# Three pieces for GpSimd's subtractions, and three later waits, in a fused attention and expert kernel

## The chip, the core and the metric

One Trainium2 chip, of which the program uses one core. The metric is the time of one execution on the device in microseconds (us); three runs of the kernel before are given, and one further execution was taken with the profiler on. The engines are named as in the profile: PE is TensorE (PEld its weight loads), DVE VectorE, ACT ScalarE, POOL GpSimd, and SP SyncE, which issues most transfers.

## The reference

Three layers follow one another, on 4 batches of 576 rows:

```python
# 1: decayed causal attention, 8 heads of 64
scores = scale * q @ k.T + (cum[:, None] - cum[None, :])   # cum: running sum of log f
attn = softmax(where(causal, -1e9, scores))
x = attn @ v                                                # heads side by side: 512 columns
# 2: mixing over rows (rank 32), then a dense layer 512 -> 2048 -> 512
u = x + (x.T @ U @ V).T
y = u + relu(u @ w_ch1) @ w_ch2
# 3: four attention experts of one head each, the best two of four per row
logits = y @ w_gate
out = sum over the chosen e of w[e] * (causal attention of y @ wq[e], y @ wk[e], y @ wv[e]) @ wo[e]
```

## The kernel before

The numbers are kept exact enough by splitting: a float32 operand becomes a high part in a narrower format and a low part that is the rest, and each product is made as high times high, high times low, low times high. So nearly every operand costs a cast on ScalarE (the high part), a subtraction (the low part), and three matmuls.

**First stage, attention (to about 260 us).** 32 heads pass through in slots of 8.4 us, two heads (a pair) per transfer of q and k. The instructions are put in order by a table of times (`put(head, us, what)`), sorted once and written out in that order for all five engines; no engine reorders. Of head h a slot holds: the score products (`sc`, L297) in two halves into the two buffers of the PSUM pool `ps2`; the exponentials (L317, ScalarE, three pieces); the high part `ph` (L322, ScalarE) and the low part (`low_part`, L325, VectorE, both operands in SBUF); the row maxima of the head two slots later (products `ua` L201 and `ub` L219 on TensorE, maxima L206 and L227 on VectorE, their transpose `mt` L233 on TensorE); and the products with the values of the head before (L353 to L357). `ub` uses the PSUM buffer of the second half of the scores, so it needs the last two exponentials done. The groups of the dense stage fill what TensorE has left.

In heads 0 to 9 the causal mask is added by a matmul; from head 10 on (`h >= 2 * NPLAIN`) the exponentials are instead cut off along the diagonal by GpSimd: `affine_select` (L1076), five per head, between the exponential and the cast `ph`. GpSimd has a second task in this stage: `split_low` (L927 to L950). q and k of a head come as float32; ScalarE makes the high parts (L895 to L899), and GpSimd subtracts them, one instruction for q and one for k, each 64 partitions by 576 columns. I call these two a set. A set is put 1.2 us behind its casts, two pairs ahead of its use, and stands in GpSimd's queue in front of the selects of the next head.

**Second stage, dense (to about 550 us).** `ffn_stream` gives groups of twelve matmuls in turn: one of the hidden layer (`hps`, L716), one of the output (`cps`, L732). `hh` (L721, ScalarE) and `hl` (L722, VectorE) make the two parts of a hidden block; `yc` (L738, VectorE) adds an output block to its sum. `hps` and `cps` share three PSUM buffers, taken in turn. Beside this stream runs a list of `jobs`, generators that `dense_one` advances by one `yield` after each group. They read the next quarter of the weights and join its bits (`narrow_quarter`: L461, L462, maximum L528), and find the power of two to scale by (`power`): maximum over columns (L540 for a weight, L592 for u), transpose `amt` on TensorE (L491), three small steps on VectorE on `ar` (L495 to L497), a matmul `rsp` that spreads the number to all partitions (L502), and the factor `es` (L504, L505). Each `yield` between these moves the next step one group later in the order of every engine. `side_factor(q, s, am)` does this for the first (s = 0) and second half of quarter q's weights; it runs for q = 2 and q = 3. `both_sides` then converts the quarter. `prepare_u(b, fy, wait)` issues the loads of batch b's u, waits `wait` groups, takes four maxima (L588), and calls `power`.

**Third stage (to the end).** The four experts; the change touches nothing of it.

Of the kernel before, what the change touches and what calls it, by code (L numbers as in the profile page):

```python
# [15 lines left out]
OP = mybir.AluOpType  # L16
# [3 lines left out]
B, H, S, D = 4, 8, 576, 64  # L20
# [18 lines left out]
UP16 = 4.0  # L39
UPW = 8192.0  # L40
# [38 lines left out]
def f32(ap):  # L79
    return ap.bitcast(F32)  # L80
# [3 lines left out]
def kernel(  # L84
# [13 lines left out]
    nc = tc.nc  # L98
# [4 lines left out]
    def pool(name, bufs=1, side="left", space=None):  # L103
        kw = {} if space is None else {"space": space}
        if space is None:
            kw["side"] = side
            kw["reuse_waits"] = "tile"
        return tc.alloc_tile_pool(name=name, bufs=bufs, **kw)
# [3 lines left out]
    ps2 = pool("ps2", 2, space=PSUM)  # L112
    ps1 = pool("ps1", 1, space=PSUM)
# [68 lines left out]
    cur = {}  # L182
# [5 lines left out]
    def drain(gen):  # L188

        while True:  # L190
            try:
                next(gen)
            except StopIteration as end:
                return end.value
# [15 lines left out]
    where = {3: (0, 0), 0: (0, 448), 2: (1, 0), 1: (1, 320)}  # L210
# [273 lines left out]
        nc.vector.tensor_tensor(back[:], sides[0][:, 0:1], sides[1][:, 0:1], OP.mult)  # L484
        scales[q] = sides, back

    def power(am, up=UP16, where=((ps1, "av"), (ps2, "s2")), pause=None):

        (p0, tag0), (p1, tag1) = where
        at_ = p0.tile([1, P], F32, name="amt", tag=tag0)  # L490
        nc.tensor.transpose(at_[:], am, ident[:])  # L491
        counter[1] += 1
        full = ars[counter[1] % 2]
        ar = full[0:1, :]
        nc.vector.tensor_reduce(ar, at_[:], AX.X, OP.max)  # L495
        nc.vector.tensor_scalar(ar, ar, 1.0e-30, None, OP.max)
        nc.vector.tensor_scalar(ar.bitcast(I32), ar.bitcast(I32), 0x7F800000, None,  # L497
                                OP.bitwise_and)
        yield pause
        yield pause  # L500
        rp = p1.tile([P, 1], F32, name="rsp", tag=tag1)
        nc.tensor.matmul(rp[:], every[:], full[:].bitcast(BF16)[:, 1:2], start=True, stop=True)  # L502
        es = cur["s16"].tile([P, 2], F32, name="es", bufs=16)
        nc.vector.tensor_scalar(es[:, 0:1], rp[:], 1.0 / up, None, OP.mult)  # L504
        nc.vector.reciprocal(es[:, 1:2], es[:, 0:1])  # L505
        return es
# [29 lines left out]
    def side_factor(q, s, am):  # L536

        yield
        a1 = cur["s16"].tile([P, 1], F32, name="wa1", bufs=2)
        nc.vector.tensor_reduce(a1[:], am[:, s, :], AX.X, OP.max)  # L540
        yield
        yield
        sides = scales[q][0]
        sides[s] = yield from power(a1[:], UPW if s else UP16)
        if s:
            back = cur["s16"].tile([P, 1], F32, name="wback", bufs=3)
            nc.vector.tensor_tensor(back[:], sides[0][:, 0:1], sides[1][:, 0:1], OP.mult)
            scales[q][1] = back

    def behind_by_one(pairs):  # L550

        last = None
        for high, low in pairs:
            high()
            if last:
                last()
            last = low
            yield
        last()
        yield  # L560
# [16 lines left out]
    def prepare_u(b, fy, wait=2):  # L577

        us = []
        for c in range(NC):  # L580
            us.append(fy.tile([P, KT, HC], F32, name="ust", tag="yc"))
            nc.sync.dma_start(us[c][:], udram[b, :, :, c * HC:c * HC + HC])
        for _ in range(wait):
            yield
        am = cur["s16"].tile([P, 2 * NC], F32, name="uam", bufs=2)
        for n in range(2 * NC):
            k = 2 * (n % 2)
            nc.vector.tensor_reduce(am[:, n:n + 1], us[n // 2][:, k:k + 2], AX.XY, OP.max,  # L588
                                    apply_absolute_value=True)
            yield  # L590
        a1 = cur["s16"].tile([P, 1], F32, name="ua1", bufs=2)
        nc.vector.tensor_reduce(a1[:], am[:], AX.X, OP.max)  # L592
        yield
        yield
        st_u[b] = us, (yield from power(a1[:]))

    def begin_u(b):

        st_u[b] += tuple(cur["fu"].tile([P, KT, S], F16, name=n + "f", tag=n) for n in ("uh", "ul"))

    def begin_sums(b, ycs):

        us, es, uh, ul = st_u[b]
        for c, yc in enumerate(ycs):
            cs = slice(c * HC, c * HC + HC)
            nc.sync.dma_start(yc[:], ydram[b, :, :, cs])
            for i, step in enumerate(steps):
                if step[:2] == (b, c) and step[2] > 0:
                    loads[i] = uh[:, :, cs], ul[:, :, cs], yc, es
# [10 lines left out]
    def convert_u(b, cs=range(NC)):  # L620
        return [u_parts(b, c, k) for c in cs for k in range(0, KT, 2)]
# [128 lines left out]
    dense, casts, sums, jobs, deferred, late = [], [], {}, [], [], []  # L750

    def ffn_prepare(i):
        if i >= QX1 or i in loads:
            return
        b, c, q, first, head, last = steps[i]
        if not head:
            loads[i] = loads[max(j for j in loads if steps[j][0:2] == (b, c))]
        else:
            loads[i] = ffn_load(b, c, first, cur["fy"])
# [112 lines left out]
    def pair_heads(p):  # L872
        return heads[2 * (p % 2)], heads[2 * (p % 2) + 1]
# [64 lines left out]
    def split_low(p, j, which=(0, 1)):  # L938

        if p >= NPAIR:  # L940
            return
        qa, qb, ka, kb = pair_heads(p)[j]
        tq, tk = places[p % 2][0][:, 0, :], places[p % 2][0][:, 1, :]
        if j == 0:
            todo = ((qb[hi_, :], tq[lo_], qa[lo_, :]), (kb[lo_, :S], tk[lo_], ka[lo_, :S]))
        else:
            todo = ((qb[lo_, :], tq[hi_], qb[hi_, :]), (kb[hi_, :S], tk[hi_], khigh[hi_, :]))
        for n in which:
            dst, src, high = todo[n]
            nc.gpsimd.tensor_tensor(dst, src, f32(high), OP.subtract)  # L950

    def one(gen):

# [489 lines left out]
    def dense_until(i):  # L1443
        while at[0] < i:
            dense_one()

    def dense_to(n):
        while groups[0] < n:
            dense_one()

    del cur["turn"]
    fu, fh, fy = cur["fu"], cur["fh"], cur["fy"]
# [12 lines left out]
    def in_turn(*gens):  # L1465
        for gen in gens:
            yield from gen

    def sums_of(p_, tags):
        return [p_.tile([P, KT, HC], F32, name="yc", tag=n) for n in tags]  # L1470
# [5 lines left out]
    def full_quarter(q, pace):  # L1476

        yield from narrow_quarter(w32[q], q, pace)
        if q == 2:
            both = wy_pool.tile([P, 4, KT, FT * P], F16, name="w16a", tag="a")  # L1480
            W[q] = [both[:, i] for i in range(4)]
        else:
            W[q] = []
            for n in ("w1h", "w1l"):
                one_ = wx_pool.tile([P, 2, KT, FT * P], F16, name=n + "f", tag=n)
                W[q] += [one_[:, i] for i in range(2)]
        jobs.append(both_sides(q))
# [8 lines left out]
    def pauses(n):  # L1496
        for _ in range(n):
            yield

    def first_quarter():  # L1500

        yield from scale_sides(1, largest[1, "sides"])
        yield from convert_weights(1)
# [4 lines left out]
    with tc.manual_schedule(engines=IN_ORDER):  # L1508
        ffn_prepare(NC * (B - 1))
        jobs.append(first_quarter())  # L1510
        jobs.append(prepare_u(0, fy2, 3))
        jobs.append(in_turn(prepare_u(1, fy2, 12)))
        jobs.append(in_turn(pauses(14), full_quarter(2, 2), pauses(8), full_quarter(3, 3)))
        dense_to(8 * (QX1 - 2) + 4)
        begin_u(0)
        begin_sums(0, sums_of(fy2, ("yc", "yc")))
        jobs.append(behind_by_one(convert_u(0)))
        dense_to(8 * (QX1 - 1) + 6)
        begin_u(1)
        jobs.append(behind_by_one(convert_u(1)))  # L1520
        begin_sums(1, sums_of(fy2, ("yc", "yc")))
        dense_until(QX1 + 5)
        jobs.append(prepare_u(2, cur["fy"]))
        dense_until(QX1 + 9)
        begin_u(2)
        begin_sums(2, sums_of(wx_pool, ("w2h", "w2l")))
        jobs.append(in_turn(behind_by_one(convert_u(2)), prepare_u(3, cur["fy"])))
        dense_until(QX1 + 11)
        begin_u(3)
        converts = behind_by_one(convert_u(3))  # L1530
        jobs.append(converts)
        dense_until(QX2)
        drain(converts)
        begin_sums(3, sums_of(cur["fy"], ("yc", "yc")))
        dense_until(QX2 + 3)
        drain(in_turn(*jobs))
        del jobs[:]
# [632 lines left out]
```

## Time and profile before

| | |
|---|---|
| three runs | 784.35, 785.31, 785.93 us (median 785.31) |
| the profiled execution | 784.53 us, of which the span from first to last instruction is 782.8 |
| PE busy | 757.9 us, 97% of the span |
| DVE busy | 601.8 us, 77% |
| ACT busy | 436.4 us, 56% |
| POOL busy | 202.9 us, 26% |
| granted TensorE clock | 0.999 of full speed |

Busy shares are means over the three stages, so they are to be read by stretches. In a timeline a row is: start, duration, engine, line, operation, what is written and read, the shapes, and how many were merged; in brackets how long the engine was idle before and what ended that. Ends of matmuls are modelled, and rows of one engine may overlap by some 0.05 us, since the next instruction starts while the last one drains.

### The profile page before, as it was taken

To read this page: it belongs to the slowest core of one execution; us is meant where nothing else is said; L and a number is where in the kernel's file an instruction comes from. 1 tells how busy PE (TensorE), PEld (TensorE's weight loads), DVE (VectorE), ACT (ScalarE), POOL (GpSimd) and SP (SyncE) were. 2 spreads that over 40 slices of the span, in tenths; PEclk is the share of its full clock that TensorE was granted. 3 is DMA by queue.
4 is the path that set the end of the run, shared out by engine and by line. 5 is a ranking of instruction groups with operands and counts; after the bars stand their busy time and mean duration, and the time that the engine had idled before them with its cause. 6 is when DMAs were issued, how large, how long until landed. Compare 5 with 4: busy or idle time off the path is not lost.

```text
span 782.8 us, 19114 instructions
## 1 busy us (share of the span) xinstructions
PE 757.9 (97%) x7312; PEld 645.3 (82%) x7312; DVE 601.8 (77%) x1662; ACT 436.4 (56%) x892; POOL 202.9 (26%) x357
## 2 busy tenths in 40 slices
PE   8898989999999999999999999999999999999997
PEld 4798989989999999877777777777778888878874
DVE  8989999999999859988773685466644688787763
ACT  7689888878787635644331242113312466786663
POOL 9842566666564200000020000000000611111110
PEclk9999999999999999999999999999999999999999
DMA  6667765665663166835223124200103475343322
GB/s 191 185 192 202 219 176 167 184 175 169 178 191 97 64 202 205 260 126 168 67 86 129 54 89 157 107 1 2 62 31 77 120 185 139 77 118 97 92 76 95
DMA packets 65688, 101.97 MB, mean 130 GB/s; under 512 B 8854, under 2 KB 43644, under 8 KB 65596
## 3 DMA queue, kind: packets, MB, share of 16 engines
q1 hardware_dynamic: 65084, 99.49, 43.3%
q8 instruction: 58, 0.95, 0.5%
q10 hardware_dynamic: 512, 1.25, 0.5%
q14 instruction: 34, 0.28, 0.1%
HBM read 53.25 MB, written 23.74 MB: 98 GB/s over the span
## 4 chain that ended last, share of the span: by engine, by line
PE 51%; DVE 3%; ACT 1%; DMA 1%; issue 0%; SPq 0%; ACTq 0%
PE cps L732 17%; PE hps L716 16%; PE pq L1668 6%; PE pv L1712 3%; PE sc L297 3%; PE po L1764 2%; PE ub L219 1%; PE av L353 1%; PE av L357 1%; PE av L355 1%; DMA ust<-udram 1%; PE pos L1764 1%; PE ua L201 0%; DVE ph L325 0%; DVE uam L588 0%
## 5 line engine op out<-in xcount | busy, mean ns | idle before, releaser
L721 ACT ACTIVATE hh<-hps 128x288 f16<-128x288 f32 (+1 forms) x128 | 52.4, 410 | 210.7 <-PE hps L716 185.7
L722 DVE SCALAR_TENSOR_TENSOR hl<-hps,hh 128x288 f16<-128x288 f32 (+1 forms) x128 | 58.2, 454 | 79.5 <-ACT hh L721 79.2
L227 DVE CUSTOM_DVE_ANT_0 ub<-ub,maskm 128x448 f32<-128x448 f32 x192 | 82.3, 429 | 1.8 <-PE ub L219 0.3
L297 PE MATMUL sc<-qa,ka 128*128 128x288 f32 (+4 forms) x288 | 72.0, 310 | 0.0
L738 DVE SCALAR_TENSOR_TENSOR yc<-cps,back,yc 128x288 f32<-128x288 f32 x96 | 49.3, 514 | 24.6 <-PE cps L732 23.0
L297 PE MATMUL sc<-qb,kb 128*128 128x288 f32 (+4 forms) x288 | 63.5, 302 | 0.0
L353 PEld LDWEIGHTS <-ph 128*128 128x128 f16 x645 | 58.9, 97 | 1.2 <-DVE o L434 0.6
L355 PEld LDWEIGHTS <-ph 128*128 128x128 f16 x645 | 59.3, 98 | 0.2
L357 PEld LDWEIGHTS <-ph 128*128 128x128 f16 x645 | 59.3, 97 | 0.0
L1896 POOL TENSOR_SCALAR_AFFINE_SELECT pf<-pf 128x128 f32<-128x128 f32 (+1 forms) x80 | 23.8, 318 | 116.4 <-ACT pf L317 115.8
L297 PEld LDWEIGHTS sc<-qb,kb 128*128 128x128 f32 x288 | 52.3, 188 | 1.5
L325 DVE TENSOR_TENSOR ph<-pf,ph 128x512 f16<-128x512 f32 (+1 forms) x66 | 47.5, 732 | 6.4 <-ACT ph L322 6.4
L206 DVE CUSTOM_DVE_ANT_0 ua<-ua,maskm 128x576 f32<-128x576 f32 x48 | 36.5, 761 | 18.8 <-PE ua L201 12.1
L325 DVE TENSOR_TENSOR ph<-aside,ph 128x512 f16<-128x512 f32 (+1 forms) x63 | 50.7, 817 | 0.1
L297 PEld LDWEIGHTS sc<-qa,ka 128*128 128x128 f32 x288 | 48.8, 190 | 2.0 <-issue 0.4
L317 ACT ACTIVATE aside<-sc 128x512 f32<-128x512 f32 (+1 forms) x63 | 38.7, 618 | 20.4 <-PE sc L297 16.9
L1076 POOL TENSOR_SCALAR_AFFINE_SELECT aside<-aside 128x128 f32<-128x128 f32 (+1 forms) x80 | 39.9, 518 | 38.3 <-ACT aside L317 28.8
L732 PE MATMUL cps<-hh,w16b 128*128 128x288 f16 x256 | 48.3, 286 | 0.3 <-DVE hl L722 0.3
L732 PE MATMUL cps<-hh,w1lf 128*128 128x288 f16 x256 | 48.4, 286 | 0.0
L732 PE MATMUL cps<-hh,w16a 128*128 128x288 f16 x256 | 48.4, 286 | 0.0
L317 ACT ACTIVATE pf<-sc 128x512 f32<-128x512 f32 (+1 forms) x66 | 39.8, 610 | 13.0 <-PE sc L297 9.4
L732 PEld LDWEIGHTS <-w16b 128*128 128x128 f16 x384 | 37.4, 98 | 10.2 <-issue 0.8
(289 smaller groups left out, 2469.5 us busy)
## 6 DMA issues: line engine op xcount, KB each, us to landing
raw<-in_w_dram SPq DMA_DIRECT2D x32, 512.0 KB
ust<-udram SPq DMA_DIRECT2D x13, 576.0 KB
ydram<-yc SPq DMA_DIRECT2D x10, 576.0 KB
aside<-in_qk_dram SPq DMA_DIRECT2D x8, 576.0 KB
udram<-ustage SPq DMA_DIRECT2D x16, 288.0 KB
ydram<-ust SPq DMA_DIRECT2D x8, 576.0 KB
yc<-ydram SPq DMA_DIRECT2D x8, 576.0 KB
room<-in_qk_dram SPq DMA_DIRECT2D x7, 576.0 KB
```

The costliest lines, as they stand in the source:

```text
L227: nc.vector.tensor_tensor_reduce(ub[:, bk, off:off + w], ub[:, bk, off:off + w], maskm[:, S - w:S], 1.0, NEG, OP.add, OP.max, mx[:, t:t + 1])
L297: nc.tensor.matmul(ps[:, bk, off:off + w], wa, xa, start=bk not in banks[:n], stop=bk not in banks[n + 1:])
L317: nc.scalar.activation(pf[:, 0:S].rearrange("p (c n) -> p c n", c=2) if whole else pf[:, 0:n], view, AF.Exp, scale=ISC)
L325: nc.vector.tensor_tensor(pl[:, o0:o0 + n], pf[:, 0:n], ph[:, o0:o0 + n], OP.subtract)
L353: nc.tensor.matmul(av[:, it, :], ph[:, c:c + P], vh[:, jt, :], start=first, stop=False)
L355: nc.tensor.matmul(av[:, it, 0:64], ph[:, c:c + P], vl[:, jt, :], start=False, stop=False)
L357: nc.tensor.matmul(av[:, it, :], pl[:, c:c + P], vh[:, jt, :], start=False, stop=last)
L716: nc.tensor.matmul(ph[:], wa[:, k, fs], xa[:, k], start=n == 0, stop=n == 3 * KT - 1)
L721: after(lambda: nc.scalar.activation(hh[:], ph[:], AF.Relu), lambda: nc.vector.scalar_tensor_tensor(hl[:], ph[:], 0.0, high, OP.max, OP.su ...
L722: lambda: nc.vector.scalar_tensor_tensor(hl[:], ph[:], 0.0, high, OP.max, OP.subtract))
L732: nc.tensor.matmul(pc[:], wa[:, t, dsl], xa[:], start=n == 0, stop=n == 3 * FT - 1)
L738: nc.vector.scalar_tensor_tensor(yc[:, d, :], pc[:], back, yc[:, d, :], OP.mult, OP.add)
```

## The change

`split_low` cuts each of its subtractions into three pieces of 192 columns, for all pairs but the first (p = 0). `power` takes the number of groups between its VectorE steps and the spreading matmul as an argument, 2 as before by default. `side_factor` for the first half of a quarter (s = 0) waits three groups instead of two in front of the transpose, and three instead of two in front of the spreading matmul. `prepare_u` for batch 2 waits four groups instead of two before its maxima.

```diff
-    def power(am, up=UP16, where=((ps1, "av"), (ps2, "s2")), pause=None):
+    def power(am, up=UP16, where=((ps1, "av"), (ps2, "s2")), pause=None, waits=2):
@@
-        yield pause
-        yield pause
+        for _ in range(waits):
+            yield pause
@@ def side_factor(q, s, am):
         nc.vector.tensor_reduce(a1[:], am[:, s, :], AX.X, OP.max)
-        yield
-        yield
+        for _ in range(2 if s else 3):
+            yield
         sides = scales[q][0]
-        sides[s] = yield from power(a1[:], UPW if s else UP16)
+        sides[s] = yield from power(a1[:], UPW if s else UP16, waits=2 if s else 3)
@@ def split_low(p, j, which=(0, 1)):
+        w = S // 3 if p else S
         for n in which:
             dst, src, high = todo[n]
-            nc.gpsimd.tensor_tensor(dst, src, f32(high), OP.subtract)
+            for c in range(0, S, w):
+                nc.gpsimd.tensor_tensor(dst[:, c:c + w], src[:, c:c + w], f32(high[:, c:c + w]),
+                                        OP.subtract)
@@
-        jobs.append(prepare_u(2, cur["fy"]))
+        jobs.append(prepare_u(2, cur["fy"], 4))
```

On GpSimd, in the head at about 122 us, a set and the selects behind it, before (`qb`, `kb` are the low parts, `aside` and `pf` the exponentials):

```order
L950 TENSOR_TENSOR qb_131<-aside,qb_131 64x576
L950 TENSOR_TENSOR kb_133<-aside,khigh 64x576
L1076 AFFINE_SELECT aside<-aside 128x128 x3
L1076 AFFINE_SELECT pf<-pf 128x128
L1076 AFFINE_SELECT pf<-pf 128x64
```

and now (all line numbers behind the change are up to three higher):

```order
L952 TENSOR_TENSOR qb_131<-aside,qb_131 64x192 x3
L952 TENSOR_TENSOR kb_133<-aside,khigh 64x192 x3
L1079 AFFINE_SELECT aside<-aside 128x128 x3
L1079 AFFINE_SELECT pf<-pf 128x128
L1079 AFFINE_SELECT pf<-pf 128x64
```

Two instructions become six, at the same place in front of the selects.

On VectorE, in the dense stage at about 374 us, the steps on `ar` for the first half of quarter 3, before:

```order
L528 TENSOR_REDUCE wam<-w_4941 128x1
L495 TENSOR_REDUCE ar_84<-amt 1x1
L496 TENSOR_SCALAR ar_84<-ar_84 1x1
L497 TENSOR_SCALAR ar_84<-ar_84 1x1
L738 SCALAR_TENSOR_TENSOR yc<-cps,back,yc 128x288
L775 TENSOR_TENSOR back<-wback,es 128x1
L722 SCALAR_TENSOR_TENSOR hl<-hps,hh 128x288
L504 TENSOR_SCALAR es<-rsp 128x1
L505 RECIPROCAL es<-es 128x1
```

and now:

```order
L528 TENSOR_REDUCE wam<-w_5061 128x1
L738 SCALAR_TENSOR_TENSOR yc<-cps,back,yc 128x288
L495 TENSOR_REDUCE ar_84<-amt 1x1
L496 TENSOR_SCALAR ar_84<-ar_84 1x1
L497 TENSOR_SCALAR ar_84<-ar_84 1x1
L775 TENSOR_TENSOR back<-wback,es 128x1
L722 SCALAR_TENSOR_TENSOR hl<-hps,hh 128x288
L738 SCALAR_TENSOR_TENSOR yc<-cps,back,yc 128x288
L461 SCALAR_TENSOR_TENSOR w_5061<-raw,w_5061 128x512
L462 SCALAR_TENSOR_TENSOR w_5061<-raw,w_5061 128x512
```

The three steps on `ar` moved behind one addition to `yc`, and the factor `es` moved out of these rows: it now stands behind a further `yc`, a block of bit joining and the `hl` after that.

On VectorE at about 393 us, the first maxima of batch 2's u (`uam`), before:

```order
L497 TENSOR_SCALAR ar_82<-ar_82 1x1
L573 SCALAR_TENSOR_TENSOR w1hf<-w_4941,es,w1hf 128x4x128
L588 TENSOR_REDUCE uam<-ust 128x1
L738 SCALAR_TENSOR_TENSOR yc<-cps,back,yc 128x288
L573 SCALAR_TENSOR_TENSOR w1hf<-w_4941,es,w1hf 128x4x128
L588 TENSOR_REDUCE uam<-ust 128x1
```

and now:

```order
L497 TENSOR_SCALAR ar_82<-ar_82 1x1
L573 SCALAR_TENSOR_TENSOR w1hf<-w_5061,es,w1hf 128x4x128
L738 SCALAR_TENSOR_TENSOR yc<-cps,back,yc 128x288
L573 SCALAR_TENSOR_TENSOR w1hf<-w_5061,es,w1hf 128x4x128
L722 SCALAR_TENSOR_TENSOR hl<-hps,hh 128x288
L504 TENSOR_SCALAR es<-rsp 128x1
L505 RECIPROCAL es<-es 128x1
L547 TENSOR_TENSOR wback<-es 128x1
L588 TENSOR_REDUCE uam<-ust 128x1
```

The first maximum, the one that needs the load, moved from behind the first conversion `w1hf` to behind the second one and the next `hl` and `es`.

## Rows read from the trace of the kernel before

**Rows 1.** Stretches: length; busy us of PE, PEld, DVE, ACT, POOL; clock; DMA.

```profile
100.00:150.00 50.00, 47.34 (x555) 44.51 (x554) 47.71 (x138) 41.06 (x82) 31.97 (x43) 1.00 0.58 168
...
500.00:550.00 50.00, 50.00 (x413) 39.93 (x412) 30.74 (x84) 11.62 (x27) 0.00 (x0) 1.00 0.00 1
```

**Rows 2.** TensorE's waits: who waited for whom, us, times, longest.

```profile
PE mt L233 <- DVE mx L227: 5.9, 10, 1.2
```

**Rows 3.** GpSimd by line and shape: count, busy us, mean ns, idle before.

```profile
L950 POOL TENSOR_TENSOR qb<-aside,qb 64x576 fp32r<-64x576 f32 x8 | 11.3, 1414 | 14.6 <-issue 7.3 <-ACT qb L898 7.1
...
L1300 POOL TENSOR_TENSOR vs<-vst,vs 32x288 fp32r<-32x288 f32 x2 | 1.6, 794 | 2.8 <-ACT vs L1296 2.7
```

**Rows 4.** One line, `low_part`: count, shortest, median, longest in ns.

```profile
L325 DVE TENSOR_TENSOR ph<-aside,ph x63: 677/765/1894, 17.3 to 270.9; 128x512 f16<-128x512 f32 x36, 128x576 f16<-128x576 f32 x27
```

**Rows 5.** Timeline of GpSimd at 122 us.

```profile
122.19 1.42 POOL L950 TENSOR_TENSOR qb<-aside,qb 64x576 fp32r<-64x576 f32 x1 [2.04 <-issue]
123.68 1.42 POOL L950 TENSOR_TENSOR kb<-aside,khigh 64x576 fp32r<-64x576 f32 x1
125.18 0.63 POOL L1076 TENSOR_SCALAR_AFFINE_SELECT aside<-aside 128x128 f32<-128x128 f32 x1
```

**Rows 6.** Timeline of VectorE at 124 us.

```profile
124.58 1.07 DVE L325 TENSOR_TENSOR ph<-pf,ph 128x512 f16<-128x512 f32 x1
125.58 0.77 DVE L325 TENSOR_TENSOR ph<-aside,ph 128x512 f16<-128x512 f32 x1
126.28 0.87 DVE L407 SCALAR_TENSOR_TENSOR vw<-room,rs,vw 128x640 f16<-128x640 f32 x1
```

**Rows 7.** Timeline of ScalarE at 126 and 150 us.

```profile
126.26 0.66 ACT L322 CAST ph<-aside 128x576 f16<-128x576 f32 x1
126.82 0.60 ACT L317 ACTIVATE pf<-sc 128x512 f32<-128x512 f32 x1
...
150.27 0.60 ACT L317 ACTIVATE pf<-sc 128x512 f32<-128x512 f32 x1
```

**Rows 8.** Timeline of TensorE at 38, 127 and 152 us.

```profile
38.19 0.27 PE L233 MATMUL mt<-ident,mx 128*5 128x128 f32 x1 [1.24 <-DVE mx L227]
...
127.49 0.45 PE L219 MATMUL ub<-ka,qa 127*128 127x448 f32 x1
...
152.04 0.53 PE L219 MATMUL ub<-ka,qa 127*128 127x448 f32 x2
```

**Rows 9.** Timeline of GpSimd: an early subtraction, and selects behind other sets.

```profile
31.40 1.41 POOL L950 TENSOR_TENSOR kb<-aside,khigh 64x576 fp32r<-64x576 f32 x1
...
157.60 1.22 POOL L1076 TENSOR_SCALAR_AFFINE_SELECT aside<-aside 128x128 f32<-128x128 f32 x2 [0.92 <-ACT aside L317]
...
175.46 0.82 POOL L1076 TENSOR_SCALAR_AFFINE_SELECT aside<-aside 128x128 f32<-128x128 f32 x1 [1.64 <-ACT mr L239]
...
243.67 0.63 POOL L1076 TENSOR_SCALAR_AFFINE_SELECT aside<-aside 128x128 f32<-128x128 f32 x1
```

**Rows 10.** Timeline of VectorE at 30 us.

```profile
31.43 1.72 DVE L407 SCALAR_TENSOR_TENSOR vw<-room,rs,vw 128x320 f16<-128x320 f32 x1
```

**Rows 11.** Timeline of TensorE in the dense stage: the four waits.

```profile
331.10 0.27 PE L491 MATMUL amt<-ident,wa 128*1 128x128 f32 x1 [0.54 <-DVE wa L540]
...
334.47 0.16 PE L502 MATMUL rsp<-ar,every 128*128 128x1 bf16 x1 [0.16 <-DVE ar L497]
...
376.60 0.16 PE L502 MATMUL rsp<-ar,every 128*128 128x1 bf16 x1 [0.52 <-DVE ar L497]
...
400.68 0.27 PE L491 MATMUL amt<-ident,ua 128*1 128x128 f32 x1 [0.23 <-DVE ua L592]
```

**Rows 12.** Timeline of VectorE in the dense stage.

```profile
330.54 0.45 DVE L722 SCALAR_TENSOR_TENSOR hl<-hps,hh 128x288 f16<-128x288 f32 x1
...
336.81 0.45 DVE L722 SCALAR_TENSOR_TENSOR hl<-hps,hh 128x288 f16<-128x288 f32 x1
...
393.94 0.75 DVE L588 TENSOR_REDUCE uam<-ust 128x1 f32<-128x576 f32 x1 [0.32 <-DMA ust<-udram]
```

## The prediction

> **What bounds the kernel now.** I read the stretches first: between 100 and 150 us TensorE is busy for 47.34 of 50 us and VectorE for 47.71, in the stretch from 500 us on TensorE for all 50 and VectorE for 30.74 [rows 1]. So the program has an attention stage (up to about 260 us) in which TensorE and VectorE both run near 95%, and a dense stage in which TensorE alone is the bound. Whatever makes TensorE stand still in either is lost for good, since nothing behind it has room to catch up. The waits of TensorE come next: the largest group is the transpose of the row maxima waiting for VectorE, 5.9 us in 10 waits [rows 2]; single ones of the attention stage are 1.24, and of the dense stage 0.54, 0.16, 0.52 and 0.23 us [rows 8, 11]. Then the timelines of GpSimd, VectorE and ScalarE around one head, which give the terms below. The span is 782.8 us and the profiled execution took 784.53; the median of the runs shown, 785.31, is 0.78 above it. My sum is made on 784.53 and shifted by 0.78 at the end.
>
> **The three waits of the dense stage.** No work is added or taken away, no transfer is issued elsewhere (the loads of u for batch 2 go out before its wait, as now), and SyncE's and ScalarE's orders stay. Four small waits of TensorE are at stake, 0.54 + 0.16 + 0.52 + 0.23 = 1.45 us [rows 11].
>
> The one at 376.60 (quarter 3): VectorE's three small steps on `ar` stand behind a block of bit joining. Now an addition to `yc` goes ahead of them (0.4 us), so they end near 376.9; TensorE asks for them two groups of twelve matmuls later, near 379. The 0.52 us goes whole. The one at 400.68 (batch 2): the four reductions start two groups later, past the landing for which VectorE idles for 0.32 us today [rows 12], and TensorE asks 2.9 us later, while VectorE only has some 2.2 us more in front; 0.23 us goes.
>
> The two at 331.10 and 334.47 (quarter 2) lie where VectorE has no idle time at all. There the wait is replaced: the output group that now comes ahead of the transpose needs the PSUM room that `hl` frees, and VectorE reads that room from 330.54 on for 0.45 us [rows 12], so TensorE goes on near 330.95 instead of 331.10. The next `hl` but one still ends near 337.2 whatever TensorE does (336.81 + 0.45 [rows 12]), and the output group behind it started at 337.44. I take 0.3 of the 0.70 us. The scale of quarter 2's first half comes some 3 us later (two groups), and ScalarE's first conversion with it may wait as long; behind it in ScalarE's queue stands the `hh` of one hidden block, which TensorE needs only two groups on, so I cost that at nothing; if that cover is gone, it is the 0.4 us by which the conversion then overlaps.
>
> Sum of the dense stage: 0.52 + 0.23 + 0.30 = 1.05 us gained; from both sides 0.3 to 1.45.
>
> **The subtractions: GpSimd's own time.** No row shows a piece of 192 columns. A subtraction of 576 columns takes 1.414 us, one of 288 takes 0.794 [rows 3]: 2.15 ns per column and 0.17 us that does not shrink, so a piece is an estimated 0.59 us. Two subtractions start 1.49 us apart [rows 5], a gap of 0.075. A set (q and k of one head) is now 2.91 us from 122.19 to 125.10, and becomes 6 x 0.59 + 5 x 0.075 = 3.9 us: 1.0 us later at its end, in 30 sets, before anyone disturbs it.
>
> **What the pieces do to VectorE.** A VectorE instruction with both operands in SBUF that meets a subtraction is held up: the `low_part` at 124.58 takes 1.07 us [rows 6], with 0.68 as the shortest and 1.89 as the longest of its kind [rows 4]. The subtraction ended 0.52 us after it began, so it loses the rest of the subtraction less 0.13 us. With pieces it meets the fourth one, 0.18 us from its end, and loses 0.05 instead of 0.39. That is the gain.
>
> But what comes next? The select at 125.18 was stretched to 0.63 us, and the `low_part` behind the first one took 0.77, 0.09 too long [rows 5, 6]: a GpSimd instruction that waits already goes in between two of VectorE's. The early rows show it at full size: the subtraction at 31.40 got in between the end of one VectorE instruction and the next, begun at 31.43, which took 1.72 us [rows 9, 10]. So piece five goes in front of the second `low_part` (it loses 0.59 less some 0.2: 0.4), and piece six in front of the `value_low` at 126.28 (0.4 again). Where three such instructions follow one another, VectorE loses 0.05 + 0.4 + 0.4 = 0.85 instead of 0.39 + 0.09; where the first meets the end of a set today it loses up to 0.4 more.
>
> The Trainium skill, page "SBUF — State Buffer", section "SBUF: two separate sides", says that GpSimd and a VectorE instruction with two SBUF inputs exclude each other, and that the loser waits until the winner's whole instruction is done. The 1.72 us row agrees with that. Taken alone the rule speaks for the change: a wait would shrink from up to 1.41 us to up to 0.59. It says nothing on how often one loses, and that is what my sum turns on; the result by the rule alone is the first rival below.
>
> **What the pieces do to the causal select.** From head 10 on the exponentials pass through a select on GpSimd, behind a set in GpSimd's queue. In the head at 122 us the select begins 0.07 us after the set, ends at 125.81, and ScalarE's cast needs it at 126.26; behind that cast stands the exponential of 126.82 to 127.42, and TensorE's `ub` product, which needs its PSUM room, starts at 127.49 [rows 5, 7, 8]. With pieces five and six each behind a `low_part` (0.68 us) the set ends near 126.75, the select then waits for the `value_low` and ends near 127.7. The cast is 1.45 us late, the exponential and `ub` as well, and TensorE stands still that long. Undisturbed by VectorE the select is 1.0 us late and the cast 0.5. I take 1.2 per head, nearer to the case in which VectorE's instructions are where the rows have them. Three heads have no idle time of GpSimd between set and select and are of this kind, at 122, 140 and 243 us (the first and the last of them are in [rows 5, 9]); at 157.60 GpSimd idled 0.92 us, which leaves 0 to 0.9, say 0.5; with 1.64 us (175.46) nothing is late [rows 9]. In the heads between, `ub` comes 1.1 us after its exponential ended (150.27 + 0.60 against 152.04 [rows 7, 8]), and that hides the delay. Sum 3 x 1.2 + 0.5 = 4.1 us lost; bounds 1.5 and 5.3.
>
> **The rest of the attention stage.** In other heads VectorE's loss counts where a wait of TensorE for VectorE stands behind it without idle time between: about three sets at 0.85 - 0.48, 1.1 us lost (bounds: 1.5 gained, 2 lost). Early, where one `value_low` has 1.72 us, 1.41 of it beside a subtraction that is over at 32.81, and a TensorE wait of 1.24 us follows at 38.19 [rows 8 to 10], the pieces save the long blocks but run on into later instructions, as the queue is then some 2 us behind: 0.3 gained (0 to 1.2). Against that stand today's waits of TensorE for VectorE: if TensorE comes later, part of the 5.9 us of [rows 2] goes. I give back 1.8 (0 to 2.5). Attention: 4.1 + 1.1 - 0.3 - 1.8 = 3.1 us lost.
>
> Total: 3.1 - 1.05 = 2.0 us lost on 784.53, 786.5; with the 0.78, **787.3 us**.
>
> **Rivals.** First, one piece per instruction: VectorE loses at most what is left of one piece, and the pieces in between find gaps. For it: many VectorE instructions in this stage (the maxima over PSUM) are not held up, so GpSimd often finds room. Against it: the select that got in between. Then VectorE's lateness, which TensorE feels as the 5.9 us of [rows 2], shrinks with the losses, such as 0.39 us at 124.58 and over 1 us at 31.43, that cause it; if 40% of those waits go, that is 2.4 us, the selects being late by less than their slack: 785.31 - 2.4 - 1.05 = 781.9 us, faster. It decides once sets end within 0.45 us of now in the three heads above.
>
> Second, a wash: sets end later and VectorE loses more, but all in slack (the 1.1 us before `ub`, VectorE's own idle time), and only the dense gain stays: 785.31 - 1.05 = 784.3. For it: ScalarE is busy for 41 of 50 us only [rows 1]. Against it: the 0.07 us between exponential and `ub` at 127.49.
>
> Third, that the change doesn't do what it says in quarter 2: VectorE without idle time turns the moved wait into another of the same length. That is inside the dense bounds, 0.4 us.
>
> **How the numbers follow.** Forecast 0.48, one piece per instruction 0.30, a wash 0.22. The forecast's own range is 785.9 to 790.3 (loss in the selects from 1.5 to 5.3, the give-back moving with it). The whole range reaches into the first rival: 781.5 to 790.3. What a measurement of this kernel can tell from no change is about 0.2%, 1.6 us, so faster is below 783.7 and slower above 786.9. Faster: 0.28 of the first rival and 0.05 of the wash, 0.33. Slower: 0.43 of the forecast. The remaining 0.24 is within 0.2%.
>
> **What would show it.** In the profile after: pieces of about 0.59 us undisturbed and sets of 3.9 to 4.7 us; `low_part` with many instructions 0.3 to 0.4 us too long and hardly any over 1.2; in the heads near 122, 140 and 243 us a cast on ScalarE that waits for the select by about a microsecond, and `ub` late with it; the TensorE waits at 376.6 and 400.7 gone. I am wrong if the sum of VectorE's `low_part` time falls, if ScalarE waits for selects no longer than before, or if the attention stage ends earlier than now.

## The result, and the profile after

The changed kernel takes 792.04 us (median of 6 runs, 789.62 to 793.30) against 785.01 for the kernel before beside it: 1.0088 of its time, 95% interval 1.0073 to 1.0103. That is 6.9 us slower by the ratio (7.0 by the two medians), where 2.0 us were forecast, and it lies above the range of 781.5 to 790.3. The profiled execution took 791.15 us with a span of 789.4, 6.6 us longer than before.

**Where the time went.** The same cast of the same head (`ph`, ScalarE) starts 1.0 us later than before near 46 us, 1.8 near 92, 2.6 near 118, 4.2 near 126, 5.9 near 142 and 8.0 from 253 us on. In the dense stage the lag shrinks to 6.8. So the attention stage lost 8.0 us and the dense stage gained 1.2. The stretches (length; busy us of PE, PEld, DVE, ACT, POOL; clock; DMA), which answer to [rows 1], show it in TensorE's 45.12 of 50 us, and a granted clock of 0.97, where the profiled execution before has 1.00:

```profile
100.00:150.00 50.00, 45.12 (x496) 42.17 (x496) 46.22 (x122) 38.02 (x76) 35.45 (x63) 0.97 0.53 152
```

The waits (who for whom: us, times, longest). ScalarE's cast waited 4.0 us in 13 places for selects in the `aside` tiles before; TensorE's `ub` waited 2.3 and 1.9 us for the two kinds of exponential, and `up`, a product of the row mixing that needs VectorE's `g`, 1.3 us in 3 places. The transposes hardly changed in sum against [rows 2]:

```profile
ACT ph L322 <- POOL aside L1079: 10.1, 19, 1.4
PE mt L233 <- DVE mx L227: 5.5, 10, 1.7
PE ub L219 <- ACT aside L317: 4.1, 4, 1.4
PE up L983 <- DVE g L971: 3.2, 7, 0.7
PE ub L219 <- ACT pf L317: 3.1, 5, 1.0
```

The pieces by themselves (count: shortest, median, longest in ns), against [rows 3], and the `low_part`s, against [rows 4]. A piece takes 0.59 us, as estimated. A set of six without disturbance takes 3.5 us and not the 3.9 of the prediction, since pieces of one tile follow each other without the gap of 0.07 us that whole subtractions have. With disturbance the 30 sets last from 3.45 to 5.11 us. The longest `low_part` is shorter than before, but 31 of the 129 now take 1.0 us or more, against 13. The first line is the one of before that [rows 4] lacks:

```profile
L325 DVE TENSOR_TENSOR ph<-pf,ph x66: 676/685/1092, 24.3 to 767.0; 128x512 f16<-128x512 f32 x50, 128x576 f16<-128x576 f32 x16
...
L952 POOL TENSOR_TENSOR qb<-room,qb x24: 584/592/607, 21.3 to 249.4; 64x192 fp32r<-64x192 f32 x24
...
L325 DVE TENSOR_TENSOR ph<-pf,ph x66: 680/748/1118, 24.3 to 773.8; 128x512 f16<-128x512 f32 x50, 128x576 f16<-128x576 f32 x16
L325 DVE TENSOR_TENSOR ph<-aside,ph x63: 680/771/1279, 17.4 to 278.8; 128x512 f16<-128x512 f32 x36, 128x576 f16<-128x576 f32 x27
```

One head of the kind that [rows 5 to 8] show, in four timelines, of GpSimd, VectorE, ScalarE and TensorE:

```profile
142.64 1.70 POOL L952 TENSOR_TENSOR qb<-room,qb 64x192 fp32r<-64x192 f32 x3 [1.48 <-issue]
144.41 2.61 POOL L952 TENSOR_TENSOR kb<-room,khigh 64x192 fp32r<-64x192 f32 x3
147.09 0.76 POOL L1079 TENSOR_SCALAR_AFFINE_SELECT aside<-aside 128x128 f32<-128x128 f32 x1
```

```profile
144.71 1.85 DVE L325 TENSOR_TENSOR ph<-aside,ph 128x512 f16<-128x512 f32 x2
146.48 1.22 DVE L407 SCALAR_TENSOR_TENSOR vw<-aside,rs,vw 128x640 f16<-128x640 f32 x1
```

```profile
147.89 0.67 ACT L322 CAST ph<-aside 128x576 f16<-128x576 f32 x1 [1.41 <-POOL aside L1079]
148.47 0.59 ACT L317 ACTIVATE aside<-sc 128x512 f32<-128x512 f32 x1
```

```profile
149.11 0.70 PE L219 MATMUL ub<-ka,qa 127*128 127x448 f32 x3 [1.34 <-ACT aside L317]
```

The set takes 4.38 us; its later pieces stand between the two `low_part`s and the `value_low`, which become 1.85 (both together) and 1.22 us long. The select ends 1.41 us too late for the cast, the exponential behind the cast is late by as much, and TensorE stands still for 1.34 us: the chain that the prediction described for the head at 122 us.

Two TensorE waits that were not foreseen, one early, one at 118 us (1.02 us before, at 116.35):

```profile
30.78 0.37 PE L297 MATMUL sc<-qa,ka 128*128 128x288 f32 x1 [2.24 <-DVE u L462]
...
118.37 0.27 PE L233 MATMUL mt<-ident,mx 128*5 128x128 f32 x1 [1.74 <-DVE mx L227]
```

The first is put down to VectorE's `u`, which the score product does not read. It does need the row of maxima that SyncE's queue brings (`qa<-mr`). The same wait in the kernel with the pieces alone (e1, below) is put down to that transfer. Here are SyncE's rows before and after, and TensorE's in e1:

```profile
24.29 0.38 SPq L877 DMA_DIRECT2D room<-in_qk_dram  x1
24.76 0.80 SPq L243 DMA_DIRECT2D qa<-mr  x1
```

```profile
25.87 0.35 SPq L877 DMA_DIRECT2D room<-in_qk_dram  x1
26.31 0.79 SPq L243 DMA_DIRECT2D qa<-mr  x1
```

```profile
30.43 0.37 PE L297 MATMUL sc<-qa,ka 128*128 128x288 f32 x1 [1.93 <-DMA qa<-mr]
```

The load of the next q and k overwrites the tile that GpSimd's set reads, so it can't be issued before the set ends: at 23.46 us before, in time for its turn, and at 25.84 now, where SyncE waits 2.0 us for it. The row of maxima stands behind that load in SyncE's queue. By the trace's semaphore records its transfer is over at 27.85 us before and at 30.65 now, 0.13 us ahead of the product. So a set has something behind it in a second queue too.

Behind the stall at 118 us the granted clock of TensorE falls to the lower of its two levels, 1.2 GHz. These are windows of 2 us with length, PE busy, clock and DMA:

```profile
116.00:118.00 2.00, 0.62 (x5) 1.00 0.90 202
118.00:120.00 2.00, 1.63 (x9) 0.75 0.63 248
120.00:122.00 2.00, 2.00 (x10) 0.50 0.43 104
122.00:124.00 2.00, 2.00 (x18) 0.90 0.46 162
124.00:126.00 2.00, 2.00 (x50) 1.00 0.00 0
```

The clock lost there is 2 x (0.25 + 0.50 + 0.10) = 1.7 us of full speed, while TensorE was nearly always busy.

In the dense stage, against [rows 11], both places of quarter 3 and batch 2 go on without a wait (386.72 and 410.40); in quarter 2 the wait is now that of an output group for `hl`, 0.47 us at 339.05 and another 0.11 at 345.32 (the 0.28 us at 335.48 stand before too, at 327.46):

```profile
335.48 0.40 PE L732 MATMUL cps<-hh,w16b 128*128 128x288 f16 x2 [0.28 <-DVE hl L722]
...
339.05 0.41 PE L732 MATMUL cps<-hh,w16b 128*128 128x288 f16 x2 [0.47 <-DVE hl L722]
...
386.72 0.17 PE L502 MATMUL rsp<-ar,every 128*128 128x1 bf16 x1
...
410.40 0.27 PE L491 MATMUL amt<-ident,ua 128*1 128x128 f32 x1
```

### The profile page after: what moved, and what is told of

It reads as the page before. It is cut to its first block, busy times and chain, and to the rows that moved or that the text cites. A ratio compares the mean times of both kernels' runs of the same rounds, so it can differ in the third digit from the quotient of the medians.

```text
span 789.4 us, 19238 instructions
## 1 busy us (share of the span) xinstructions
PE 760.0 (96%) x7312; PEld 647.0 (82%) x7312; DVE 608.4 (77%) x1662; ACT 437.8 (55%) x892; POOL 232.6 (29%) x477
## 3 DMA queue, kind: packets, MB, share of 16 engines
q10 hardware_dynamic: 512, 1.25, 0.5%
## 4 chain that ended last, share of the span: by engine, by line
PE 53%; DVE 2%; ACT 1%; issue 0%; ACTq 0%
PE cps L732 17%; PE hps L716 16%; PE pq L1671 6%; PE pv L1715 3%; PE sc L297 3%; PE po L1767 2%; PE ub L219 1%; PE av L353 1%; PE av L357 1%; PE av L355 1%; PE pos L1767 1%; PE ua L201 0%; DVE ph L325 0%; PE mt L233 0%; ACT pf L317 0%
## 5 line engine op out<-in xcount | busy, mean ns | idle before, releaser
L325 DVE TENSOR_TENSOR ph<-pf,ph 128x512 f16<-128x512 f32 (+1 forms) x66 | 50.4, 777 | 6.4 <-ACT ph L322 6.4
L325 DVE TENSOR_TENSOR ph<-aside,ph 128x512 f16<-128x512 f32 (+1 forms) x63 | 54.2, 872 | 1.0 <-ACT ph L322 0.9
```

The costliest lines, as they stand in the source:

```text
L325: nc.vector.tensor_tensor(pl[:, o0:o0 + n], pf[:, 0:n], ph[:, o0:o0 + n], OP.subtract)
```

## The experiments

Each kernel was timed against the kernel before on the same chip; an interval in brackets is the 95% interval of the ratio. e2 and e11 are written as edits of the changed kernel, the others of the kernel before. They are named e1 to e12 in the order of the record.

**Four kernels that take the change apart.** The first has the pieces alone (`split_low` as changed), the second the waits alone (all of the change but `split_low`). The third and the fourth have the pieces for some pairs only:

```diff
+        w = S // 3 if 1 <= p < 7 else S     # e3; in e4: if p >= 7
```

> The pieces for all pairs but the first, the three waits as before. Forecast's reading (the loss is the pieces', the dense waits gain): the changed kernel lost 0.88%, 6.9 us, with the dense stage falling from 8.0 us behind to 6.8 behind; so this kernel is 6.9 + 1.2 = 8.1 us slower than before, and its dense stage has the waits of 331.1, 334.5, 376.6 and 400.7 us again, 8 us later. Rival (the moved waits themselves cost, the pieces are cheap): under 5 us slower.

Measured 791.86 us against 784.43: 7.4 us slower [1.0073, 1.0102]. The loss is the pieces', by a little less than expected; of the four waits that were to come back, the one of 400.7 us did not.

> The three later waits, the subtractions whole as before. Forecast's term: 1.05 us faster (0.3 to 1.45); by the trace of the changed kernel 1.2. Rival (the waits gain only because the dense stage starts later there, with other transfers in flight): no change, within 0.3 us.

Measured 783.18: 1.25 us faster [0.9974, 0.9998]. Up to 253 us its trace runs within 0.06 us of before, so no other start of the dense stage is needed for the gain. The lag goes to -0.13 us behind quarter 2, -0.81 behind quarter 3 and -1.21 behind batch 2: 0.13, 0.68 and 0.40 us, where the forecast had 0.30, 0.52 and 0.23.

> Waits as before; pieces only for pairs 1 to 6, 12 of the 30 sets, all of which run before the first head with a select. Theory 1 (selects that come late are the main loss): 1 to 1.5 us slower at most, since no select stands behind a set in pieces. Theory 2 (each set in pieces costs VectorE about 0.2 us wherever it stands, and VectorE and TensorE have no room): 12/30 of 8.1, so 3.2 us slower. By the forecast's own early term: 0.3 us faster.

Measured 785.85: 1.4 us slower [1.0011, 1.0029], the upper end of theory 1. The sign of the forecast's early term is wrong.

> Waits as before; pieces only for pairs 7 to 15, 18 of the 30 sets, all of which run among the heads with selects. Theory 1 (selects): 6.5 to 7 us slower, nearly the whole loss. Theory 2 (turns with VectorE, wherever): 18/30 of 8.1, so 4.9 us slower. If the granted clock drops to half for about 3 us behind a stall of TensorE near 117 us as in the changed kernel, 1.6 us of this is the clock's.

Measured 790.62: 6.2 us slower [1.0049, 1.0080]. 12 sets without selects cost 1.4 us and 18 with them 6.2; the sum, 7.6, is about that of e1. That speaks for theory 1, but it is no proof, since the heads differ in more than the selects. The worst head of its profiled execution, in the timelines of GpSimd, ScalarE and TensorE:

```profile
142.96 3.29 POOL L952 TENSOR_TENSOR kb<-room,khigh 64x192 fp32r<-64x192 f32 x3
146.32 0.29 POOL L1079 TENSOR_SCALAR_AFFINE_SELECT aside<-aside 128x128 f32<-128x128 f32 x1
```

```profile
146.64 0.67 ACT L322 CAST ph<-aside 128x576 f16<-128x576 f32 x1 [1.90 <-POOL aside L1079]
```

```profile
147.86 0.62 PE L219 MATMUL ub<-ka,qa 127*128 127x448 f32 x2 [1.83 <-ACT aside L317]
```

Three pieces that take 1.7 us undisturbed took 3.29 between three VectorE instructions, and TensorE stood still for 1.83 us. The clock fell behind this stall too (0.50 from 150 to 152 us), and behind one of 1.83 us at 116.94.

**Place, number, and delay alone.** e5 and e6 put the sets of pairs 7 to 15 behind the selects of the next head, with pieces and whole; e7 has two pieces at the old place; e8 leaves the subtractions alone and delays what stands behind them.

```diff
-            put(h, us + 1.2, split_low, p, j)
+            put(h, us + 1.2 if p < 7 else SLOT + 2.8, split_low, p, j)   # e5, e6
...
+        w = S // 3 if p >= 7 else S         # e5; in e7: S // 2; e6: S
...
+        if p >= 7:                          # e8, behind the subtractions
+            for _ in range(9):
+                nc.gpsimd.memset(cur["idle"][:], 0.0)
```

> Waits as before; pieces for pairs 7 to 15 as in e4_pieces_with_selects (6.2 us slower), but each of those sets stands behind the five selects of the next head in GpSimd's queue instead of in front of them. Theory 1 (a set in pieces ends later, the selects behind it come late, ScalarE's cast and TensorE's ub product with them): nearly all of the 6.2 us goes, 0 to 1.5 us slower than before. Theory 2 (more turns between GpSimd and VectorE cost the time, wherever the set stands): 4 to 6 us slower, as e4.

Measured 781.73 against 784.49: 2.76 us faster [0.9944, 0.9975]. The same pieces, 9 us better than in e4 by their place alone. Theory 2, the cost wherever the set stands, falls. But the new place differs in two things, what stands behind the set and what VectorE does beside it; e8 parts the two. GpSimd around one set:

```profile
127.02 1.05 POOL L1079 TENSOR_SCALAR_AFFINE_SELECT pf<-pf 128x128 f32<-128x128 f32 x2 [0.29 <-ACT pf L317]
128.15 1.72 POOL L952 TENSOR_TENSOR qb<-aside,qb 64x192 fp32r<-64x192 f32 x3
129.93 1.72 POOL L952 TENSOR_TENSOR kb<-aside,khigh 64x192 fp32r<-64x192 f32 x3
```

Here VectorE reduces row maxima out of PSUM, and the six pieces run through in 3.50 us. The `low_part`s, in the page's list of groups (count | busy us, mean ns | idle before), first of the changed kernel and then of e5; before they are 50.7 and 47.5 us:

```profile
L325 DVE TENSOR_TENSOR ph<-aside,ph 128x512 f16<-128x512 f32 (+1 forms) x63 | 54.2, 872 | 1.0 <-ACT ph L322 0.9
L325 DVE TENSOR_TENSOR ph<-pf,ph 128x512 f16<-128x512 f32 (+1 forms) x66 | 50.4, 777 | 6.4 <-ACT ph L322 6.4
```

```profile
L325 DVE TENSOR_TENSOR ph<-aside,ph 128x512 f16<-128x512 f32 (+1 forms) x63 | 47.6, 767 | 0.1
L325 DVE TENSOR_TENSOR ph<-pf,ph 128x512 f16<-128x512 f32 (+1 forms) x66 | 46.7, 720 | 6.4 <-ACT ph L322 6.4
```

The sums are 98.2 us before, 104.6 after, 101.0 in e4 and 94.3 in e5. So the same pieces lengthen VectorE's `low_part`s at the old place, beside runs of them, by 2.8 us (e4). That e5 has less than before is nearly all the place: with whole subtractions there (e6, next) the sum is 95.1.

> Waits as before, subtractions whole; sets of pairs 7 to 15 behind the selects of the next head. Separates what the place alone does from what the pieces do there. Theory 1: the selects of before wait for sets too (ScalarE's cast waits 4.0 us for them in 13 places), so 0.5 to 1.5 us faster than before. Theory 2: no change, within 0.5 us; the difference to e5 would be the price of the pieces without selects behind them, by theory 2 4 to 6 us, by theory 1 under 2.

Measured 782.86: 1.6 us faster [0.9964, 1.0002], just short of being told from no change. The place alone gives about this much; the pieces there are another 1.1 us by the medians, with intervals that overlap.

> As e4_pieces_with_selects, with two pieces of 288 columns in place of three of 192. By the lengths of rows of before (0.794 and 1.414 us) a set grows by about 0.5 us instead of 0.9 to 1.0. Both theories: between before and e4; in proportion to the added length 3 us slower. If only the number of turns counted, also half. If the drop of the clock decides (it came where TensorE stood still for more than 1.7 us), under 2 us, since the stalls stay shorter.

Measured 786.51: 2.0 us slower [1.0011, 1.0032]. A set is 3.46 us long on average here, 4.09 in e4 and 2.92 before, so 0.54 us more cost 2.0 us and 1.17 us more cost 6.2: more than in proportion, as long as e4's falls of the clock are counted in (without them it is 4.5, see e8, which is in proportion). In its profiled execution only one stall among the heads with selects (1.15 us) was above 1.04 and the clock stayed at full speed, which is close to the third of the expectations (under 2 us).

> Waits as before, subtractions whole and in their place; behind each set of pairs 7 to 15 nine small fills of 32 x 16 by GpSimd, in front of the selects, about 0.95 us in all (estimated from the fills of 32x128 and 32x576, 0.20 and 0.57 us). It delays the selects as the pieces do, without further subtractions for VectorE to meet. Theory 1 (late selects): 4 to 6 us slower. Theory 2 (turns with VectorE): under 1.5 us slower.

Measured 787.25: 2.8 us slower [1.0023, 1.0048], between the two theories. The nine fills took 1.37 us, not 0.95. GpSimd, ScalarE and TensorE in the head shown of e4:

```profile
142.20 1.37 POOL L954 MEMSET idle<- 32x16 f32 x9
143.64 0.60 POOL L1080 TENSOR_SCALAR_AFFINE_SELECT aside<-aside 128x128 f32<-128x128 f32 x1
```

```profile
144.27 0.67 ACT L322 CAST ph<-aside 128x576 f16<-128x576 f32 x1 [1.37 <-POOL aside L1080]
```

```profile
145.50 0.47 PE L219 MATMUL ub<-ka,qa 127*128 127x448 f32 x1 [1.29 <-ACT aside L317]
```

A delay without one further subtraction makes the same kind of wait, 1.29 us here against 1.34 in the changed kernel and 1.83 in e4, and VectorE's `low_part`s hardly grow (99.4 us in sum). So late selects alone cost TensorE time. But a uniform 1.37 us costs 2.8 us and the pieces, with 1.17 on average, 6.2. The rest comes from the sets that VectorE stretches most (5.08 us at 141 us in e4), and from the clock: e4's two runs with a mean granted clock of 0.998 or more took 788.8 and 789.1 us, its three with 0.996 from 790.6 to 792.3. So of the 6.2 us about 4.5 are there at full clock.

**The two worst sets.** e9 is e4 with the second sets of pairs 7 and 9 whole:

```diff
+        w = S // 3 if p >= 7 and (p, j) not in ((7, 1), (9, 1)) else S
```

> As e4_pieces_with_selects (6.2 us slower), with two of its 18 sets whole again: the second of pair 7 and the second of pair 9, behind which TensorE stood still 1.83 us at 116.94 and 1.83 us at 147.86 and its granted clock fell to half for some 3 us each. Clock theory: with the stalls back near 1.0 and 0 us the clock stays at full speed, which gives back 0.8 + 1.8 us of stall and 2 x 1.6 us of clock, so about 0.5 us slower than before. Without the clock (time behind a stall is not lost by it, TensorE having slack there): 2.6 us back at most, 3.6 us slower than before. Shared equally over the sets: 2/18 of 6.2, so 5.5 us slower.

Measured 787.52 against 784.47: 3.05 us slower [1.0030, 1.0055]. Two sets of 18 carried half of e4's loss, the falls of the clock behind them included, so it is not shared equally. By the numbers this is nearest to the line without the clock (3.6), and my expectation by the clock was too large. The other 16 sets cost about what the uniform delay of e8 did (2.8). As an estimate from these medians, of e4's 6.2 us about 1.7 are the clock's, 1.5 those of the two worst sets at full clock, and 3.0 the rest. The profiled execution gives back more: at 150 us it is 1.3 us behind before, where e4 was 6.0 behind, and of these 4.7 us only 0.8 + 1.8 are stalls; its clock does not fall. TensorE at the two places:

```profile
116.51 0.27 PE L233 MATMUL mt<-ident,mx 128*5 128x128 f32 x1 [1.04 <-DVE mx L227]
...
144.06 0.76 PE L219 MATMUL ub<-ka,qa 127*128 127x448 f32 x4
```

Both fit together if the clock does not fall in every execution of e4, which its mean clocks suggest but no second trace shows: the profiled one, 792.32 us with two falls, was the longest of its five.

**The early part, and the two gains together.**

```diff
+        w = S // 3 if p in (1, 2) else S    # e10
...
+        w = S // 3 if 1 <= p < 7 else S     # e12
+            put(h, us + 1.2 if p < 2 or p >= 7 else SLOT + 2.8, split_low, p, j)
```

> Pieces for pairs 1 and 2 alone, 4 sets, all over by about 45 us. In e3_pieces_before_selects (1.4 us slower) the loss stood at 0.57 us by 46 us, 1.0 by 76 and 1.4 by 100. If each part of it has its own set: 0.6 us slower, and the score product at 30 us waits for VectorE as there. If the later parts follow from the early one (a queue that is late from there on): 1.4 us. By the forecast's early term: 0.3 us faster.

Measured 784.97 against 784.47: 0.5 us [0.9999, 1.0017], not to be told from no change by itself; its trace is 0.65 us behind from 46 us to the end of the attention stage. By the trace, then, each part of the early loss has its own sets. The product at 30 us does not wait for VectorE, as the expectation has it, but for the late row of maxima: its transfer is over at 30.34 us and the product starts at 30.47.

> As e3_pieces_before_selects (pieces for pairs 1 to 6), with the sets of pairs 2 to 6 put 5.1 us later, at the place that e5 uses for the later pairs; no select is near them but for the last. If the early loss comes from what the pieces meet on VectorE at their place (the low parts of the exponentials and the steps behind them, up to the product up that waits for g): the 0.8 us behind 46 us go, 0.6 us slower than before. If it comes from their number of turns: 1.4 us slower as e3.

Measured 787.50: 3.0 us slower [1.0028, 1.0053], worse than e3. Up to 76 us its trace is 0.75 us behind (e3: 1.0); then 2.3 us more are lost by 103. At the seam a moved set and the next, unmoved one come one after the other, in front of the first selects. GpSimd there, and TensorE:

```profile
97.56 1.74 POOL L952 TENSOR_TENSOR kb<-aside,khigh 64x192 fp32r<-64x192 f32 x3
99.37 1.42 POOL L952 TENSOR_TENSOR qb<-room,qa 64x576 fp32r<-64x576 f32 x1
100.86 1.76 POOL L952 TENSOR_TENSOR kb<-room,ka 64x576 fp32r<-64x576 f32 x1
102.58 2.16 POOL L1079 TENSOR_SCALAR_AFFINE_SELECT aside<-aside 128x128 f32<-128x128 f32 x3
```

```profile
104.58 0.48 PE L219 MATMUL ub<-ka,qa 127*128 127x448 f32 x1 [0.66 <-ACT pf L317]
```

I had not seen that when I built it. By itself it leaves its question open, what the early pieces meet, and shows late selects once more. The traces answer it for the first part: the product at 30 us waits 1.61 us here as well, for the row of maxima behind the load that waits for pair 1's set, and that set was not moved.

e11 is the changed kernel with pieces for pairs 7 to 15 only and those sets put as in e5.

> The three later waits, pieces only for pairs 7 to 15 and those sets behind the next head's selects: e2 and e5 together. If their gains stand in different stages and add up: 1.25 + 2.76 = 4.0 us faster than before. If the dense gain hangs on when that stage starts: 2.8 to 3.5.

Measured 780.43: 4.04 us faster [0.9940, 0.9965]. The gains add up, and this version beats both kernels.

## Why the prediction was wrong

**The dense stage: right.** Forecast 1.05 us gained, measured 1.25 (e2). In quarter 2 the 0.54 and 0.16 us became 0.47 and 0.11, so less was gained there than the 0.30 of the sum, and more behind it (0.68 and 0.40 us for 0.52 and 0.23), which stays unexplained. ScalarE's first conversion for quarter 2 waits 2.7 us, as foreseen; no wait of TensorE stands behind it.

**The selects: right in mechanism, somewhat too large.** Forecast 4.1 us. The `ub` waits of the heads with selects in the profile after are 0.44 at 131.68, 1.34 at 149.11, 1.36 at 166.31, 0.82 at 237.29 and 0.43 at 254.22, 4.4 us in all, where before had 0.34 in these heads and 1.02 in one whose wait is gone: 3.0 us more. That the 4.4 is so near to 4.1 is luck. The three heads put at 1.2 each (122, 140 and 243 us) have 0.44, 1.34 and 0.43, the head at 157 us, put at 0.5, has 1.36, and a head of the kind called covered has 0.82. The signs that the prediction named came true: longer `low_part`s, ScalarE's casts that wait, the waits at 376.6 and 400.7 us gone.

**The step that failed is the rest of the attention stage**, "4.1 + 1.1 - 0.3 - 1.8", whose last three terms make 1.0 us gained. In the profiles they are 2.5 us lost:

| term | forecast | profile after against before |
|---|---|---|
| `ub` behind late selects | 4.1 lost | 3.0 lost |
| early part (to 92 us) | 0.3 gained | 1.8 lost |
| VectorE's lateness later on, less the waits given back | 1.1 - 1.8: 0.7 gained | 0.7 lost |
| TensorE busy for longer | no term | 2.4 lost |
| dense stage | 1.05 gained | 1.25 gained |
| sum | 2.0 lost | 6.7 lost |

The early wait at 38.19 us went, 1.24 gained, as the prediction said. But for these heads it knew only VectorE as touched by late pieces. The load that waits for the set's tile, and the row of maxima behind that load, made the new wait of 2.24 us at 30.78, and two waits of `up` add 0.7. The kernel with early pieces alone (e3) lost 1.4 us. The 1.8 us were to come back because TensorE, being later, would wait less for row maxima. The wait went from 5.9 to 5.5 us, and without the early 1.24 it rose from 4.7. What came back is two waits of an `amt` transpose, 1.1 us. VectorE is late by the same sets that make the selects late (`low_part`: 6.4 us more in sum), and at 118 us the wait for it grew from 1.02 to 1.74.

**What was missing in the sum is the clock.** Of the 2.4 us that TensorE was busy for longer, the 1.7 us computed above are the clock's; 0.7 stay open. How often the clock falls varies: the six runs of the changed kernel have a mean granted clock of 0.995 to 0.997. Of the 66 runs of the kernel before that stand beside the experiments, 56 are at 0.998 or above (median 784.4), eight at 0.997 (median 786.1, 1.7 more), and two at 0.992 and 0.990 (788.4 and 790.7). With the pieces alone (e1) one run at 0.999 took 790.4 and three at 0.996 or 0.997 from 791.7 to 792.5. So the clock belongs to the loss, in e1 with some 1.5 us, but most of the loss is there without it.

**The first rival, one piece per instruction,** did not decide here, and e5, the kernel nearest to it, gains by it only the 0.8 us of `low_part` time by which it differs from e6. The Trainium skill, page "SBUF — State Buffer", section "SBUF: two separate sides", has the loser wait for the winner's whole instruction. The longest `low_part` fell from 1.89 to 1.28 us, as that rule says, while their sum rose by 6.4 us; by these runs what decides is how often a piece finds a two-operand instruction beside it. The wash fell with the 7.4 us of e1; the third rival, the moved wait in quarter 2, came true within its bounds.

## What to carry to other kernels

Before cutting a background engine's instruction into pieces, look at what stands behind it in its own queue, and at who waits for the tiles that it reads: the set as a whole gets longer, and whatever waits behind it pays, a load in another engine's queue and what is queued behind that load included, while the engine it was to spare meets it more often. Moving the whole block behind the urgent work, where the other engine also reads elsewhere, was worth more than either size of piece at the old place (e5 against e4: 9 us). And where two engines get later by the same cause, do not book the waits of a third one on them as time given back.

## What was not expected of the hardware

The clock's fall is not settled by the stall ahead of it. It fell behind stalls of 1.74 us (after), 1.84 (e1) and 1.83 twice (e4), not behind 1.34 and 1.36 us (after) or 1.60 (e6, at 232.93), but neither behind the 2.24 us at 30.78. In e3 and e10 it fell at about 25 us, where the stall ahead, at 22.7, was 0.94 us; e12 and the changed kernel have the same stall there and no fall. In e10, windows as above:

```profile
22.00:24.00 2.00, 1.28 (x10) 1.00 0.32 65
24.00:26.00 2.00, 2.00 (x15) 0.78 0.28 82
26.00:28.00 2.00, 2.00 (x15) 0.50 0.56 187
28.00:30.00 2.00, 1.53 (x41) 0.86 0.81 237
```

What decides stays open. Nor does a fall always cost what it takes: behind this one the wait for the row of maxima at 30 us is 0.71 (e3) and 0.94 us (e10), where the traces without a fall there have 1.61 (e12), 1.93 (e1) and 2.24 (after). So part of what the slower clock took there came out of a wait that stood behind it.

Small GpSimd fills follow each other more slowly than their length: nine of 32x16, 101 ns each, start 0.16 us apart, so that they took 1.37 us together.
